# Two gated spectral filters on one core: the second branch's inverse units are divided by output rows, run in halves by kind of product, and the whole plan is written anew

## The chip, the cores and the metric

The kernel runs on one core of one Trainium2 chip. The metric is the time of one execution on the device in microseconds (us), the median of several runs, lower being better.

## What is computed

One image `x` of 2048 rows and 1024 columns goes through two spectral filters with different weights. A gate, one number for each row of the image, mixes the two results.

```python
def _ref(x, w_r, w_i):                       # once with A's weights, once with B's, both on x = A_x
    X = jnp.fft.rfft2(x.astype(jnp.float32), axes=(-2, -1))
    X = X * (w_r + 1j * w_i)                 # 2048 x 513
    return jnp.fft.irfft2(X, s=(2048, 1024), axes=(-2, -1)).astype(jnp.bfloat16)

g = sigmoid((x * gate_w).sum(-1, keepdims=True))
out = g * a + (1 - g) * b
```

## The kernel before

The row of the image is 16 p + n2: partition p holds 16 rows, n2 = 0 to 15. All transforms are matmuls with constant matrices, and every matmul result is evicted from PSUM by ACT (line 417) or DVE (line 418). The stages:

1. **S1, Z, gate.** The columns of x are folded into sums and differences on DVE (`fS`, `fT`, `f2`, line 395). For each n2 a matmul group S1 makes the first part of the transform over the rows, and its eviction Z goes to the buffer TV. A small group `gfold` needs the constants MS, which the DMA `c_MS` brings (ACT's queue), and the gate's weights, which `gwr` reverses on ACT. Its eviction `g8` feeds the groups `gate`, whose rows `zrow` are evicted and summed (`zg`).
2. **D, S2.** Sixteen groups D, number 4 sq + j, transform the columns; they read all of Z. Their evictions Q lie in the ring, 8 cells for each sq. For each sq two groups S2 finish the transform over the rows, evicted as X into the buffer R4: 16 slots s, of which sq covers four, with two parts of 513 each.
3. **Products.** For each branch b (0 is A, 1 is B) and each sq, DVE makes four products of X with the weights (`mul`, `prod`): two kinds (o = 0 with the real weights, o = 1 with the imaginary ones), each in two halves h of two slots. `ploc` says where each product lies. Kind 1 overwrites its weights in WAB. Kind 0 goes into the upper half of TV for A. For B it goes where A's products of kind 1 lay, so it waits until A's units have read those.
4. **Inverse units I.** A wide unit (`stage_iw`, I1W, 32 matmuls) takes half of the slots of one sq and makes a part of all 16 output rows n2. A narrow unit (`stage_i1`, I1, 64 matmuls) takes all slots of one sq and makes one half of the output rows: th = 0 gives n2 0 to 7 (lower), th = 1 gives n2 8 to 15 (upper). `WIDE` lists which (b, sq) are wide. Each unit fills two pairs of PSUM banks, evicted as two tiles V (j = 0, 1) into the ring, 2 of its 28 cells each. From there a DMA of 256 KB, the *turn*, carries the tile across partitions into TV: A's part over Z, B's part over A's products of kind 0. So there are 16 units, 32 evictions V and 32 turns. A ring cell is free again when its turn has landed.
5. **Tail.** For each output row n2, S1A reads A's part and S1B reads B's part of TV, with the gate folded into the constants FM and RM (`sig`, `RA`, `RB`); S1H is both in one group. The eviction G goes to R4, Di2 (or Di) transforms the columns, its eviction `o` goes to WAB, and DVE unfolds in steps u, e and y. A DMA on SP's queue writes each pair of rows. `vkeys` says on which turns a row n2 waits: all turns of wide units, and the turns of narrow units of its own half.

Nothing is scheduled at run time. `Plan` numbers all steps (nodes) in the order in which the program adds them. Three strings, ORDER, ENGS and CELLS, give the order in which they are issued, the engine of each, and the place of each tile in PSUM or ring. A planner wrote these strings beforehand. Each engine runs its steps in that order, and so do the two queues that issue DMAs, POOL and SP. `Sched` sets the waits.

In the order before, the wide units are all of A's and B's sq 3. PE runs the units in the order (b, sq, and half): 0,1,1 | 0,1,0 | 0,0,1 | 0,2,1 | 0,0,0 | 0,2,0 | 0,3,0 | 0,3,1 | 1,0,0 | 1,0,1 | 1,3,1 | 1,2,0 | 1,1,0 | 1,3,0 | 1,1,1 | 1,2,1, the first two ahead of the last two D groups, the first four ahead of the last S2 group. After these come S1A of the rows 2, 0, 3 and 1, and S1B of 3, 2, 1 and 0. The DMA `c_MS` is ACT's second step, `gwr` follows the load of the activation table, and `c_DI` (512 KB of constants for Di) is issued by SP ahead of all turns. Of B's narrow units, SP issues the turn of j = 0 and POOL that of j = 1; POOL issues all turns of wide units.

Of the kernel before, what the change touches and what calls it, by code (L numbers as in the profile page):

```python
# [19 lines left out]
PAIRS = {"warm": 12, "S2": 16, "I1": 64, "I1W": 32, "S25": 8, "gate": 8, "zg": 4, "gm": 8}  # L20
DEPTH = ((0, 2), (2, 4), (4, 6), (6, 8), (8, 10), (10, 12), (12, 14), (14, 16))
ORDER = (
    "020b0h030c000i04010506070n0j080m090f0a0g0d0q0s0e0o0t0r0k0y0w0p0z0u0l24140x15100v251b12111a181h131g1c19261o1e1p1d16271q1f"
    "1r2s28171w1s1u1i1t292v1x1v1j2a1z1m2w1k1y2t2b1n1l22202c232u212y2x2z2d3o3m2e3p3b3n2f3s3c2g3q3t372h3r31382i403u3239422j412q"
    "303v3a33352k343w3x362l493z3y2m434a3d5n3g2n445p3e3i2o473h3f45482p5o3j464o5q3k4p4b3l4h4i4j4e4c5b4f4k4d4g4l5w2r5c5r5x635z59"
    "4q5u4m774r5y644n5i605s5v5a5t4y5l4s6v5j5m4t614u4z5k6a6w50624v6d6b4x6e7n4w6c5d6h655e6f5g5f6i55665h516g56676t686j527o696o6m"
    "6u6k6n7z6r6l6x816p6s7l6q726y82706z7m757188737976747p788b8c7a7s897q7t7b808a7r57837c7e7d587f7g86538454877j857u7h7k7i8u7v7x"
    "8d7w8z7y8i908v918j8w8e8k928x8f938l8y8g8m9b94958h979f969c9u8n8o9g9q988q9v9d9r9h9e9w8p9i9s99a59x8r9a9ja99t9k8saia69l8t9yam"
    "aa9z9ma7aja09nabana1aka89oaoac9palava2apazaeawa3b8aqb0a4axadb9arbab1afaybdasbmb2agatbbahbeb4boaubcbibrbhbnb3bsbfbpbgb5bq"
    "bvb6bub7btbjbwbkbxblbybz")  # L30
ENGS = (
    "sadsadpsasssdasdsasaspdspdapdpadpagdadpagdpadpdadpagdpdapgdadpgadppdagpdadgdpapdagdappgdpappagppgdpagpdgpapgapdgpddpagds"
    "ppappgddpagpdagpaddpgadpagpdapagdpapdaaddpadppdapadapsdpadadpapdagdapgagdgpaddagpdaagpdadpadagdagpdpadagdpagpdagdapadgpa"
    "dagdagpdagdgpadasdagpadgspdagdadagpdgsdpadsdgpadadgagpagspadpspgpppapdpappadpapapddadpdapddapddapdpapdapdpadsdpaddpadsdp"
    "addpaddpadpadpdsapdapdadpdaspdadapdapdpaddpsadasadpdadadpddadddsdddddsds")
CELLS = (
    "071052794002440d28404702486402463204060846204g62402640g027420648g02461204260204406624gij7062402062446086002462460284602a"
    "0244668c026042a264680402ac60402046400824264002c406408248a060424c0460280g424078064867c60046")


def bf16_bits(a):
# [309 lines left out]
def bass_gated_mix__spectral_gfnet__spectral_gfnet__prompt_kernel(  # L351
# [289 lines left out]
    def ploc(b, o, cx, s):  # L641
        if o:
            return WAB, (2 * b + 1 - cx) * WH + s * WP
        if b:
            return WAB, cx * WH + s * WP
        return TV, 16384 + s * 2 * NS + cx * NS

    def prod(b, sq):
        P.key = ("P", b, sq)
        for h in range(2):  # L650
            s0 = 4 * sq + 2 * h
            x = ap(R4, s0 * 2 * NS, [[2 * NS, 2], [NS, 2], [1, NS]])
            r = [("X", s0 + i, c) for i in range(2) for c in range(2)] + [("X5", sq)] + wk[b]
            for o in range(2):
                w = ap(WAB, (2 * b + o) * WH + s0 * WP, [[WP, 2], [(WH, -WH)[o], 2], [1, NS]])
                if o:
                    d, old = w, [("P", b, sq, 0, h)]
                elif b:
                    d, old = ap(WAB, s0 * WP, [[WP, 2], [WH, 2], [1, NS]]), [("P", 0, sq, 1, h)]
                else:  # L660
                    d, old = ap(TV, 16384 + s0 * 2 * NS, [[2 * NS, 2], [NS, 2], [1, NS]]), allf
                P.add("mul", vt(2048), lambda e, w=w, d=d, x=x: [tt(d, x, w, ALU.mult)], r, [("P", b, sq, o, h)], after=old)

    def stage_i1(b, sq, th):
        P.key = ("I", b, sq, th)
        v = [Tile("v", 2), Tile("v", 2)]
        t = [Tile("ps", 2), Tile("ps", 2)]
        pk = [("P", b, sq, o, h) for o in range(2) for h in range(2)]

        def fns():  # L670
# [12 lines left out]
        old = [("P", 0, q, 0, h) for q in range(4) for h in range(2)] if b else allz  # L683
        pt = pit[id(TV)]
        for j in range(2):
            ev("V", 1024, lambda j=j: (rg(v[j], 0, [[1, 1024]]), psl(t[j], 0, [[1, 1024]])),
               [(t[j],)], [(v[j], 0, 2)], alloc=[v[j]])
            dma("turn", ("sp", "pool")[j], lambda j=j: [(AP(TV, (64 * j + sq) * pt + b * 16384 + th * 1024, [[4 * pt, 16], [2048, 8], [1, 1024]]),
                                                         rg(v[j], 0, [[1, 1024]]))], 0.262, 118, [(v[j], 0, 2)], [("V", b, sq, th, j)], after=old)

    def stage_iw(b, sq, a):
        P.key = ("I", b, sq, a)
        v = [Tile("v", 2), Tile("v", 2)]
        t = [Tile("ps", 2), Tile("ps", 2)]

        def fns():
            f = []
            for pr in range(4):
                for c in range(2):
                    for i in range(2):  # L700
                        T, off = ploc(b, pr // 2, pr % 2, 4 * sq + 2 * a + i)
# [5 lines left out]
        pe("I1W", [512] * 8 + [64], fns, [("P", b, sq, o, a) for o in range(2)] + ["SK"], [(t[0],), (t[1],), ("I1", b, sq, a)], alloc=t)  # L707
        old = [("P", 0, q, 0, h) for q in range(4) for h in range(2)] if b else allz
        pt = pit[id(TV)]
        for j in range(2):  # L710
            ev("V", 1024, lambda j=j: (rg(v[j], 0, [[1, 1024]]), psl(t[j], 0, [[1, 1024]])),
               [(t[j],)], [(v[j], 0, 2)], alloc=[v[j]])
            dma("turnw", "pool", lambda j=j: [(AP(TV, (64 * j + 32 * a + sq) * pt + b * 16384, [[4 * pt, 8], [1024, 16], [1, 1024]]),
                                               rg(v[j], 0, [[1, 1024]]))], 0.262, 118, [(v[j], 0, 2)], [("V", b, sq, "w", a, j)], after=old)

    for sq in range(4):
        for j in range(4):
# [39 lines left out]
    allx = [("X", s, c) for s in range(16) for c in range(2)] + [("X5", i) for i in range(4)]  # L757
    oldw = [("P", 1, sq, o, h) for sq in range(2) for o in range(2) for h in range(2)] + \
           [k for b in range(2) for k in wk[b]]

    def tail(ns):
        k = len(ns)
        o, e, y = Tile("o", 2 * k), Tile("e", 2 * k), Tile("y", 2 * k)
        for r, n2 in enumerate(ns):
# [6 lines left out]
                pe("S1H", [128] * 16, lambda n2=n2, t=t: s1inv(n2, t), vkeys(n2), [(t,)], alloc=[t])  # L771
            if k == 1:
                for c in range(2):
                    ev("G", 512, lambda n2=n2, t=t, c=c: (ap(R4, n2 * 1024 + c * 512, [[1, 512]]), psl(t, c * 512, [[1, 512]])),
                       [(t,)], [("G", n2, c)], after=allx)
            else:
                ev("G", 1024, lambda n2=n2, t=t: (ap(R4, n2 * 1024, [[1, 1024]]), psl(t, 0, [[1, 1024]])),
                   [(t,)], [("G", n2, c) for c in range(2)], after=allx)

            def di(c, t, n2=n2):  # L780
                f = []
                for par in range(2):
                    for hh in range(2):
                        l = ap(R4, n2 * 1024 + c * 512 + par * 256 + hh * 128, [[1, 128]])
# [88 lines left out]
```

## Time and profile before

| what | us |
|---|---|
| runs shown | 124.15, 126.17, 126.38 |
| their median | 126.17 |
| span of the profiled execution | 124.9 |
| busy in the span: PE, DVE, ACT, POOL | 103.4, 99.5, 96.5, 41.6 |

The page's header says how long the profiled execution took from its first to its last instruction. That span is 1.3 us below the median of the runs, and one run lies below it. PE is the matmul engine, and a busy PE is not one at its peak. No engine is busy throughout, so the share of each stage matters, not the mean. Times below count from the start of the span.

### The profile page before, as it was taken

Reading aid. Unit: us, or ns where it says so; the run is one execution under the profiler, and the core shown is the slowest. Engines: PE = TensorE matmul, PEld = TensorE weight load, DVE = VectorE, ACT = ScalarE, POOL = GpSimd, SP = SyncE. Lnnn points to the kernel's source line nnn. Section 1 sums busy time; section 2 is a strip of 40 time slices with the busy share of each in tenths; the row PEclk is TensorE's granted clock in tenths of the full one; section 3 lists DMA queues with packets and bytes.
Section 4 is the critical chain, followed back from the end, with each engine's and each line's share of the span. In section 5 each row is a group of like instructions: output and inputs, shape, how many; then the busy total and the mean of one; then the engine's idle time right before and its main releaser. Section 6 shows DMA issues by size and latency. Waiting matters only on the chain.

```text
span 124.9 us, 3644 instructions
## 1 busy us (share of the span) xinstructions
PE 103.4 (83%) x1588; PEld 71.7 (57%) x1588; DVE 99.5 (80%) x134; ACT 96.5 (77%) x111; POOL 41.6 (33%) x74
## 2 busy tenths in 40 slices
PE   6799979999999999785969965896499999999610
PEld 2288836977764556333524322432389999999400
DVE  0479999458699997999999999480307899999991
ACT  4499999466999879994989695673519999999930
POOL 0007699999990003613334331333100000000000
PEclk9999999999999999999999999999859999999975
DMA  4999999999999972898675789889680004444456
GB/s 106 407 419 411 385 336 235 341 338 322 321 293 293 247 212 58 227 168 199 183 182 160 172 205 259 219 190 225 203 243 7 0 5 168 168 173 168 198 220 253
DMA packets 10881, 27.85 MB, mean 223 GB/s; under 512 B 4305, under 2 KB 4305, under 8 KB 10610
## 3 DMA queue, kind: packets, MB, share of 16 engines
q0 software_dynamic: 6688, 15.25, 45.2%
q1 hardware_dynamic: 4032, 12.36, 28.2%
q8 instruction: 12, 0.20, 0.6%
q10 hardware_dynamic: 146, 0.02, 0.1%
q14 instruction: 3, 0.02, 0.1%
HBM read 15.01 MB, written 4.19 MB: 154 GB/s over the span
## 4 chain that ended last, share of the span: by engine, by line
DVE 33%; DMA 22%; PE 22%; ACT 14%; issue 5%; SPq 1%; DVEq 0%; ACTq 0%
PE PS L392 22%; DMA TV<-RING 18%; DVE RING L395 18%; ACT RING L417 9%; DVE WAB L395 9%; DMA WAB<-in_A_x_dram 4%; DVE R L418 3%; ACT R L417 2%; DVE TV L395 2%; DVE RING L418 1%; ACT TV L417 1%; ACT FM L729 1%; ACT WAB L417 1%; SPq L426 1%; DVE WAB L418 0%
## 5 line engine op out<-in xcount | busy, mean ns | idle before, releaser
L417 ACT ACTIVATE RING<-PS 128x1024 bf16<-128x1024 f32 x41 | 40.2, 1026 | 15.0 <-PE PS L392 8.2
L395 DVE TENSOR_TENSOR WAB<-R,WAB 128x2052 bf16<-128x2052 bf16 x24 | 28.1, 1225 | 0.7 <-DMA WAB<-in_B_w_i_dram 0.6
L395 DVE TENSOR_TENSOR RING<-WAB 128x1024 bf16<-128x1024 bf16 (+1 forms) x42 | 23.9, 608 | 5.3 <-DMA WAB<-in_A_x_dram 4.5
L417 ACT ACTIVATE R<-PS 128x1024 bf16<-128x1024 f32 (+2 forms) x29 | 24.6, 937 | 4.3 <-PE PS L392 4.2
L426 POOL DMA_DIRECT2D TV<-RING x26 | 15.2, 586 | 37.1 <-ACT RING L417 20.2
L392 PE MATMUL PS<-WAB,SK 64*32 64x512 bf16 (+1 forms) x576 | 23.4, 377 | 3.4 <-ACT RING L417 3.4
L392 PEld LDWEIGHTS PS<-WAB,SK 64*32 64x32 bf16 (+1 forms) x576 | 10.5, 97 | 15.0 <-ACT RING L417 6.2
L392 PE MATMUL PS<-FM,TV 128*128 128x128 bf16 x128 | 14.5, 237 | 3.1 <-ACT RING L417 3.1
L392 PE MATMUL PS<-DM,TV 128*128 128x256 bf16 x128 | 15.5, 274 | 0.3 <-ACT TV L417 0.3
L392 PEld LDWEIGHTS PS<-FM,TV 128*128 128x128 bf16 x128 | 13.6, 120 | 3.8 <-ACT RING L417 3.8
L418 DVE CAST RING<-PS 128x1024 bf16<-128x1024 f32 x7 | 8.6, 1223 | 9.0 <-PE PS L392 4.9
L418 DVE CAST R<-PS 128x1024 bf16<-128x1024 f32 (+1 forms) x9 | 9.9, 1105 | 6.6 <-PE PS L392 6.5
L392 PEld LDWEIGHTS PS<-DM,TV 128*128 128x128 bf16 x128 | 13.3, 115 | 2.3 <-issue 1.2
L417 ACT ACTIVATE WAB<-PS 128x1024 bf16<-128x1024 f32 (+1 forms) x16 | 14.5, 1014 | 0.2 <-PE PS L392 0.2
L392 PE MATMUL PS<-DI,R 128*128 128x256 bf16 (+1 forms) x128 | 13.4, 260 | 1.1 <-ACT R L417 1.1
L417 ACT ACTIVATE TV<-PS 128x1024 bf16<-128x1024 f32 x14 | 13.3, 1040 | 0.5 <-PE PS L392 0.5
L392 PE MATMUL PS<-TV,RING 128*128 128x256 bf16 (+1 forms) x128 | 12.3, 253 | 1.7 <-DVE RING L395 0.8
L392 PE MATMUL PS<-RM,TV 128*128 128x128 bf16 x128 | 13.4, 222 | 0.0
L392 PEld LDWEIGHTS PS<-RM,TV 128*128 128x128 bf16 x128 | 12.9, 115 | 0.0
L392 PEld LDWEIGHTS PS<-TV,RING 128*128 128x128 bf16 x128 | 10.3, 98 | 4.3 <-DVE RING L395 2.2
L392 PEld LDWEIGHTS PS<-DI,R 128*128 128x128 bf16 x128 | 11.0, 98 | 2.6 <-ACT R L417 1.6
L392 PE MATMUL PS<-TV,SK 64*64 64x512 bf16 x128 | 8.4, 381 | 4.4 <-DVE RING L418 1.8
(41 smaller groups left out, 97.9 us busy)
## 6 DMA issues: line engine op xcount, KB each, us to landing
TV<-RING POOLq DMA_DIRECT2D x26, 256.0 KB, 6.0
WAB<-in_A_x_dram SPq DMA_DIRECT2D x8, 512.0 KB, 7.3
out_dram<-RING SPq DMA_DIRECT2D x7, 512.0 KB, 2.6
TV<-RING SPq DMA_DIRECT2D x6, 256.0 KB, 6.0
WAB<-in_A_w_r_dram POOLq DMA_DIRECT2D x2, 513.0 KB, 9.8
WAB<-in_A_w_i_dram POOLq DMA_DIRECT2D x2, 513.0 KB, 9.0
WAB<-in_B_w_r_dram POOLq DMA_DIRECT2D x2, 513.0 KB, 8.7
WAB<-in_B_w_i_dram POOLq DMA_DIRECT2D x2, 513.0 KB, 12.1
```

Source lines behind the costliest of these rows:

```text
L392: return lambda e: e.matmul(o, l, r, start=start, stop=stop, skip_group_check=True)
L395: return lambda e: e.tensor_tensor(out=o, in0=a, in1=b, op=op)
L417: return [lambda e: e.activation(o, i, ACT.Copy)]
L418: return [lambda e: e.tensor_copy(o, i)]
L426: n = P.add(name, es, lambda e: [lambda q, d=d, s=s: q.dma_start(d, s) for d, s in pairs()], reads, writes, dma=kind, **kw)
L729: P.add("sig", {"act": (0.92, 1.12)}, lambda e, f=f, t=t: [lambda e: e.activation(f, psl(t, 0, [[1, 1024]]), ACT.Sigmoid)], [(t,)], [("gr" ...
```

## The change

Four things change in the program text.

- `WIDE` loses (1, 3). All eight units of branch B are now narrow, so four of them make only lower rows and four only upper rows. `vat` lays B's rows in TV one after the other. A lower turn of B then covers only the place of A's products of sq 0 and 1, an upper turn that of sq 1 to 3 (`dead`).
- A narrow unit is issued as two nodes of 32 matmuls, first the products of kind 0, then those of kind 1, and each waits for its own kind alone. They share their PSUM tiles, and their matmuls are those of before.
- B's products of kind 0 of the slots 8 to 15 go to the lower half of R4, where X of the slots 0 to 7 lay, and not into WAB.
- The inverse rows G of n2 0 to 7 go to the upper half of R4, those of n2 8 to 15 to the upper halves of the first two parts of WAB (`grow`), with the waits of `oldg`. `oldw` no longer names the loads of the weights.

The cut diff:

```diff
-WIDE = ((0, 0), (0, 1), (0, 2), (0, 3), (1, 3))
+WIDE = ((0, 0), (0, 1), (0, 2), (0, 3))
...
         if b:
-            return WAB, cx * WH + s * WP
+            return (WAB, cx * WH + s * WP) if s < 8 else (R4, (2 * s - 16 + cx) * NS)
...
+                elif b and sq > 1:
+                    d = ap(R4, (s0 - 8) * 2 * NS, [[2 * NS, 2], [NS, 2], [1, NS]])
+                    old = [("X", s0 - 8 + i, c) for i in range(2) for c in range(2)] + [("X5", sq - 2)]
...
+    def vat(b, n2):
+        return b * 16384 + (n2 if b else n2 % 8 * 2 + n2 // 8) * 1024
+
+    def dead(b, th):
+        return [("P", 0, q, 0, h) for q in ((0, 1), (1, 2, 3))[th] for h in range(2)] if b else allz
...
-            for pr in range(4):
+            for pr in (2 * o, 2 * o + 1):
...
-        pe("I1", [512] * 8 + [64], fns, pk + ["SK"], [(t[0],), (t[1],), ("I1", b, sq, th)], alloc=t)
+        for o in range(2):
+            pe("I1", [512] * 4 + [64], lambda o=o: fns(o), [("P", b, sq, o, h) for h in range(2)] + ["SK"], [(t[0],), (t[1],)], alloc=t if o == 0 else [])
...
+    def grow(n2, off, n):
+        t, at = (R4, 16 * NS + n2 * 1024) if n2 < 8 else (WAB, (n2 // 4 - 2) * WH + 8 * WP + n2 % 4 * 1024)
+        return ap(t, at + off, [[1, n]])
```

The strings ORDER, ENGS and CELLS are new from end to end. Read against the list of nodes they give these orders, as far as they bear on the text below:

- **Front.** ACT: gw, table, two FN, Z 0, Z 1, gwr, Z 3, `c_MS`, Z 2, Z 5, Z 6, Z 7, g8, Z 4, Z 8, Z 9, Z 13, Z 12, Z 11, Z 15. PE: S1 of 0, 1, 2, 3, 5, 6, 4, 7, then gfold, then S1 of 8, 9, 13, 12, 10, 11, 14, 15, gate 0, gate 2, then D. DVE sets the 8 zeros that `table` reads after the first fold. Two of three `zrow` go from ACT to DVE, and gate 1, gate 3 and the four `zg` come later, among the D groups.
- **D and S2.** PE: D 3, 2, 12, 0, 1, 5, 4, S2 of sq 0, D 6, 7, S2 of sq 0, D 14 and so on. All D and S2 groups now come before the first unit. The last D is D 8; three S2 groups follow it. The first product is (0, 0). Between the first product and the last, DVE also evicts three X and one Q, and one `zrow`, but no V (before: four X, two V).
- **Units on PE:** 0,0,1 | 0,1,0 | 0,1,1 | 0,3,0 | 0,0,0 | 1,1,0 | 0,2,0 | 1,1,1 | 0,3,1 | 0,2,1 | 1,0,0 | 1,3,0 | 1,2,0 | 1,0,1 | 1,3,1 | 1,2,1. The two `gm` groups of the gate stand between the halves of 1,3,0. The last two products are (1, 2), kinds 0 and 1 of h = 1. S1A of the rows 3, 1, 0, 2 and S1B of 1, 2, 3, 0 follow the last unit.
- **V.** DVE evicts one of the two tiles of 1,3,0, both of 1,0,1, and one each of 1,3,1 and 1,2,1, with `RA` and `RB` between them. ACT evicts the other 27.
- **Turns on SP:** 1,3,0 | 1,0,0 | 1,1,0 | 1,2,0, then `c_DI`, then 1,1,1 | 1,0,1 | 1,3,1 | 1,2,1, all j = 0. **On POOL:** 18 turns (the 16 of branch A, and j = 1 of 1,1,0 and 1,0,0), then j = 1 of 1,2,0 | 1,3,0 | 1,0,1 | 1,3,1 | 1,1,1 | 1,2,1.
- **Cells.** Thirteen tiles V stand on places that no turn holds, a fourteenth place is kept for the last tile of 1,2,1, and every other tile waits for an earlier turn. The tiles of 1,3,1 wait for POOL's 16th and 18th turn. The first `y` step (rows 2 and 3), DVE's twelfth step of the tail, takes the cells of that last tile of 1,2,1, so it waits for SP's last turn.

More of the change, by code (lines that the diff above doesn't have):

```diff
@@ L22 @@
 ORDER = (
[L23 to L30, printed above, removed]
+    "02030405060708090a0h0n000m0s0t0y0z14151b1a1h1g0i0b010f0g0o0p0q0u0w0r0j0x0c0v121316101718190k1c0l111e1d1f1p1j1o1x1q1r1w1i"
@@ L667, in stage_i1, with fns @@
         t = [Tile("ps", 2), Tile("ps", 2)]
-        pk = [("P", b, sq, o, h) for o in range(2) for h in range(2)]
-        def fns():
+        def fns(o):
             f = []
-            for pr in range(4):
+            for pr in (2 * o, 2 * o + 1):
                 for c in range(2):
@@ L687, in stage_i1 @@
                [(t[j],)], [(v[j], 0, 2)], alloc=[v[j]])
-            dma("turn", ("sp", "pool")[j], lambda j=j: [(AP(TV, (64 * j + sq) * pt + b * 16384 + th * 1024, [[4 * pt, 16], [2048, 8], [1, 1024]]),
-                                                         rg(v[j], 0, [[1, 1024]]))], 0.262, 118, [(v[j], 0, 2)], [("V", b, sq, th, j)], after=old)
+            dma("turn", ("sp", "pool")[j], lambda j=j: [(AP(TV, (64 * j + sq) * pt + vat(b, 8 * th), [[4 * pt, 16], [(2048, 1024)[b], 8], [1, 1024]]),
+                                                         rg(v[j], 0, [[1, 1024]]))], 0.262, 118, [(v[j], 0, 2)], [("V", b, sq, th, j)], after=dead(b, th))
     def stage_iw(b, sq, a):
@@ L706, in fns @@
             return f
-        pe("I1W", [512] * 8 + [64], fns, [("P", b, sq, o, a) for o in range(2)] + ["SK"], [(t[0],), (t[1],), ("I1", b, sq, a)], alloc=t)
-        old = [("P", 0, q, 0, h) for q in range(4) for h in range(2)] if b else allz
+        pe("I1W", [512] * 8 + [64], fns, [("P", b, sq, o, a) for o in range(2)] + ["SK"], [(t[0],), (t[1],)], alloc=t)
         pt = pit[id(TV)]
@@ L713, in stage_iw @@
             dma("turnw", "pool", lambda j=j: [(AP(TV, (64 * j + 32 * a + sq) * pt + b * 16384, [[4 * pt, 8], [1024, 16], [1, 1024]]),
-                                               rg(v[j], 0, [[1, 1024]]))], 0.262, 118, [(v[j], 0, 2)], [("V", b, sq, "w", a, j)], after=old)
+                                               rg(v[j], 0, [[1, 1024]]))], 0.262, 118, [(v[j], 0, 2)], [("V", b, sq, "w", a, j)], after=dead(b, 0) + dead(b, 1))
     for sq in range(4):
@@ L755, in vkeys, with oldg @@
                 for x in ((("w", 0), ("w", 1)) if (b, sq) in WIDE else ((n2 // 8,),))] + [(("RA", "RB")[b], n2 // 8) for b in bs]
-    allx = [("X", s, c) for s in range(16) for c in range(2)] + [("X5", i) for i in range(4)]
-    oldw = [("P", 1, sq, o, h) for sq in range(2) for o in range(2) for h in range(2)] + \
-           [k for b in range(2) for k in wk[b]]
+    oldw = [("P", 1, sq, o, h) for sq in range(2) for o in range(2) for h in range(2)]
+    def grow(n2, off, n):
+        t, at = (R4, 16 * NS + n2 * 1024) if n2 < 8 else (WAB, (n2 // 4 - 2) * WH + 8 * WP + n2 % 4 * 1024)
+        return ap(t, at + off, [[1, n]])
+    def oldg(n2):
+        if n2 < 8:
+            return [("X", s, c) for s in range(8, 16) for c in range(2)] + [("X5", i) for i in (2, 3)]
+        return [("P", 0, sq, 1, h) for sq in (2, 3) for h in range(2)]
     def tail(ns):
@@ L773, in tail @@
                 for c in range(2):
-                    ev("G", 512, lambda n2=n2, t=t, c=c: (ap(R4, n2 * 1024 + c * 512, [[1, 512]]), psl(t, c * 512, [[1, 512]])),
-                       [(t,)], [("G", n2, c)], after=allx)
-            else:
-                ev("G", 1024, lambda n2=n2, t=t: (ap(R4, n2 * 1024, [[1, 1024]]), psl(t, 0, [[1, 1024]])),
-                   [(t,)], [("G", n2, c) for c in range(2)], after=allx)
+                    ev("G", 512, lambda n2=n2, t=t, c=c: (grow(n2, c * 512, 512), psl(t, c * 512, [[1, 512]])),
+                       [(t,)], [("G", n2, c)], after=oldg(n2))
+            else:
+                ev("G", 1024, lambda n2=n2, t=t: (grow(n2, 0, 1024), psl(t, 0, [[1, 1024]])),
+                   [(t,)], [("G", n2, c) for c in range(2)], after=oldg(n2))
             def di(c, t, n2=n2):
```

24 lines of the change are left out of this document (15 added, 9 removed).

## The prediction

> **What bounds the kernel now.** I cut the span where the work changes hands: the start of the D groups (22.06), the first product (33.64), the end of the last one (78.04, where the next DVE step starts), the first S1B (92.54) and the end of DVE (122.33). The windows view gives each stretch: length, busy time of the five engines with instruction counts, granted clock, DMA share, GB/s.
>
> ```profile
> span 124.9 us, 3644 instructions
> PE 103.4 (83%) x1588; PEld 71.7 (57%) x1588; DVE 99.5 (80%) x134; ACT 96.5 (77%) x111; POOL 41.6 (33%) x74
> ...
> 0.00:22.06 22.06, 18.81 (x180) 12.81 (x181) 16.39 (x26) 18.26 (x23) 10.97 (x23) 1.00 0.94 328
> 22.06:33.64 11.58, 11.58 (x132) 9.50 (x133) 6.95 (x10) 7.49 (x9) 11.58 (x20) 1.00 1.03 333
> 33.64:78.04 44.40, 36.77 (x670) 19.41 (x668) 43.69 (x42) 37.19 (x42) 15.07 (x26) 1.00 0.81 206
> 78.04:92.54 14.50, 10.74 (x256) 6.28 (x257) 5.03 (x7) 7.40 (x8) 3.96 (x7) 0.90 0.85 218
> 92.54:122.33 29.79, 25.54 (x354) 23.69 (x352) 27.47 (x52) 26.13 (x32) 0.00 (x0) 0.96 0.34 131
> ```
>
> PE fills the second stretch (11.58 of 11.58), DVE the third (43.69 of 44.40), DVE and ACT together the fifth. In the fourth no engine is full, and DMA is at 0.85. The chain of waits (start, us, what) tells what the fourth waits for:
>
> ```profile
> 82.06 7.63 DMA TV<-RING
> ...
> 89.78 1.03 ACT RING L417
> 90.86 2.56 PE PS L392 x24
> ```
>
> The timeline (start, us, instruction, idle before it and what ended that) shows the same from PE and DVE:
>
> ```profile
> 78.04 0.69 DVE L395 TENSOR_TENSOR FM<-RM,FM 128x1024 bf16<-128x1024 bf16 x1
> 78.55 5.63 PE L392 MATMUL PS<-WAB,SK 64*32 64x512 bf16 x160 [1.77 <-ACT RING L417]
> 84.37 1.92 PE L392 MATMUL PS<-WAB,SK 64*32 64x512 bf16 x64 [0.19 <-ACT RING L417]
> 87.76 1.22 DVE L418 CAST RING<-PS 128x1024 bf16<-128x1024 f32 x1 [4.06 <-DMA TV<-RING]
> 89.14 1.49 PE L392 MATMUL PS<-FM,TV 128*128 128x128 bf16 x16 [2.85 <-ACT RING L417]
> 90.86 1.89 PE L392 MATMUL PS<-FM,TV 128*128 128x128 bf16 x16 [0.22 <-ACT RING L417]
> 92.54 2.20 PE L392 MATMUL PS<-RM,TV 128*128 128x128 bf16 x32
> ```
>
> After the last product four units remain. Their evictions wait for ring cells, cells wait for turns of some 7.6 us, and S1A waits for PSUM behind those evictions (2.85). S1B starts right behind S1A: it waits for PE, not for landings. From S1B on, 32.3 us remain (92.54 to 124.85). So the end is S1B's start plus the tail.
>
> **The change, term by term.** The sum is made against the profiled execution, span 124.9; the median of the runs is 126.17, and I carry the difference over to it.
>
> *Term 1, the front: +1.5.* The counts of S1, folds and evictions stay. ACT takes in `gwr` and the issue of `c_MS` and gives two `zrow` to DVE:
>
> ```profile
> 1.28 0.37 ACTq L426 DMA_DIRECT2D MS<-c_MS  x1
> 3.09 1.04 ACT L494 ACTIVATE R<-R 1x1024 bf16<-1x1024 bf16 x1
> 7.25 1.94 ACT L417 ACTIVATE TV<-PS 128x1024 bf16<-128x1024 f32 x2 [0.19 <-PE PS L392]
> 9.43 9.31 ACT L417 ACTIVATE TV<-PS 128x1024 bf16<-128x1024 f32 x10 [0.17 <-PE PS L392]
> 18.62 1.09 ACT L417 ACTIVATE FM<-PS 128x512 bf16<-128x512 f32 x2
> ...
> MS<-c_MS ACTq DMA_DIRECT2D x1, 16.0 KB, 4.6
> DM<-c_DM SPq DMA_DIRECT2D x1, 512.0 KB, 13.6
> ```
>
> That is 1.04 + 0.37 - 1.09 = +0.3. The wait is worth more. `gwr` ended at 4.13, well ahead of the first Z; now Z 0, Z 1, `gwr` and Z 3 stand ahead of `c_MS`, which is issued at about 7.25 + 1.9 + 1.0 + 0.3 = 10.5 instead of 1.28. At 4.6 us it lands at 15.1; PE can run `gfold` at about 13.7, as its PSUM is free after Z 5, three evictions of 0.93 later. Behind `gfold` stand all further S1 on PE, and behind `g8` on ACT eight evictions Z. From `g8` on, ACT needs 0.2 + 7 x 0.93 = 6.7 to the last Z (ten take 9.31), and D reads every Z. I take 5.9 us for `c_MS`, between its own 4.6 and the 13.6 of a constant queued under load, much nearer to 4.6 as it is 16 KB on a queue of its own. It lands at 16.4, and D starts at 16.4 + 0.5 + 6.7 = 23.6, 1.5 late. Bounds: 0 (landing hidden) and +9 (13.6 us, D at 31). The zeros for `table` now follow a fold, which costs 0.7 at most and is inside these bounds.
>
> *Term 2, D to the first product: 0.* Before, 11.6. After, nine D and two S2 groups come ahead of the X that the first product needs:
>
> ```profile
> 22.06 5.40 PE L392 MATMUL PS<-DM,TV 128*128 128x256 bf16 x48 [0.35 <-ACT TV L417]
> 27.39 0.61 PE L392 MATMUL PS<-TV,G 128*32 128x512 bf16 x8
> 27.94 1.06 PE L392 MATMUL PS<-RING,SK 64*64 64x512 bf16 x16
> 29.83 0.24 PE L392 MATMUL PS<-MS,FM 128*128 128x1 bf16 x4
> 30.00 0.29 PE L392 MATMUL PS<-RING,SK 128*64 128x2 bf16 x8
> 32.43 1.23 DVE L418 CAST R<-PS 128x1024 bf16<-128x1024 f32 x1 [1.64 <-PE PS L392]
> 33.64 2.37 DVE L395 TENSOR_TENSOR TV<-R,WAB 128x2052 bf16<-128x2052 bf16 x2
> ```
>
> 9 x 0.9 + 2 x 0.95 + 1.2 for the eviction + 0.3 = 11.5. First product at 35.1.
>
> *Term 3, first to last product: -2.2.* DVE is the bound here:
>
> ```profile
> 48.21 3.51 DVE L395 TENSOR_TENSOR WAB<-R,WAB 128x2052 bf16<-128x2052 bf16 x3 [0.64 <-DMA WAB<-in_B_w_i_dram]
> 60.82 15.03 DVE L395 TENSOR_TENSOR WAB<-R,WAB 128x2052 bf16<-128x2052 bf16 x13
> ```
>
> A product or an eviction takes 1.15 (13 in 15.03). The 32 products stay. Six evictions (four X, two V) become four plus one `zrow` (half the columns, taken as 0.7): -2.3 + 0.7. The 0.64 for B's weights goes, since B's first product now follows thirteen of A's and comes well after 48. The new home in R4 has the same shape, so it costs nothing if its readers are done: it waits for products that stand earlier on DVE itself. Bounds: -2.9 and 0 (a product that waits for a unit of A). The last product ends at 77.3.
>
> *Term 4, last product to S1B: -3.3.* Before, 14.5. After: the second half of 1,2,0 (0.95); 1,0,1 and 1,3,1 (1.88 each, three units in 5.63); 1,2,1, whose PSUM is free only when DVE has evicted both tiles of 1,0,1 with `RA` between (1.2 + 0.7 + 1.2 against 1.9 on PE: 1.0 lost); 1.88; four S1A and a wait of 0.2 (3.6). Sum 11.2, so S1B at 88.5. Two covers must hold.
>
> First, ring cells. All D and S2 groups now precede the units: 16 x 0.9 + 8 x 0.95, and 3.4 for four Nyquist groups, two gates and four `zg` (0.29, 0.61, 0.24) make 25.4. With the unit (1.9) and its eviction (0.9) the first tile stands at D + 28.2 = 51.8.
>
> ```profile
> 48.80 1.79 POOL L426 DMA_DIRECT2D TV<-RING  x3 [11.34 <-PE PS L392]
> 71.25 20.10 SPq L426 DMA_DIRECT2D TV<-RING  x6
> ...
> 52.00:60.00 8.00, 5.54 (x104) 2.71 (x107) 8.00 (x8) 5.96 (x8) 2.39 (x4) 1.00 0.89 190
> 75.00:79.00 4.00, 2.23 (x82) 0.97 (x74) 3.73 (x4) 2.53 (x3) 0.83 (x2) 1.00 0.98 240
> ...
> TV<-RING POOLq DMA_DIRECT2D x26, 256.0 KB, 6.0
> DI<-c_DI SPq DMA_DIRECT2D x1, 512.0 KB, 3.4
> RM<-c_RM SPq DMA_DIRECT2D x1, 512.0 KB, 10.3
> ```
>
> So turns begin 3.0 later than at 48.80. A turn is 262 KB: 1.38 us at the 190 GB/s that POOL alone moved, 1.09 at the 240 of POOL and SP together. POOL's 18th turn lands near 51.8 + 6 + 17 x 1.38 = 81.3, and 1,3,1 needs its cell at 82.
>
> Second, landings of the lower rows. SP holds the j = 0 tiles of 1,1,0 and 1,0,0 back behind 1,3,0, whose tiles come at 77. So at 77.3 four lower turns go out on SP and some two remain on POOL; with what moves beside them, eight turns, 9 to 11 us and some 2 to land: 88 to 90, against 88.5. The upper turns end later, and S1A, S1B and the first Di2 cover them. That is the gain: before, S1B came after every unit's eviction had found its cell. Bounds of term 4: -4.3 (DVE costs PE nothing) and +1.5 (no overlap of the queues).
>
> *Term 5, the tail: +0.5.* Counts on DVE and ACT are the same (one eviction swapped). Two new waits: the first Di2, 2 us behind S1B at 90.5, needs `c_DI`, issued near 81 among the turns. It landed in 3.4 on quiet queues; its twin `c_RM` took 10.3 under load. And the first `y` step, some 9 us into the tail, needs SP's last turn: some 17 transfers from 77.3 at 1.1 to 1.38 end between 96 and 101, against 97.5. Bounds 0 and +3.
>
> *Sum:* 1.5 + 0 - 2.2 - 3.3 + 0.5 = -3.5. Span 121.4; median 126.17 - 3.5 = 122.7.
>
> **The rivals.**
> - *`c_MS` is not late* (landing by 14.5, term 1 is +0.3): 121.5 (122.7 - 1.2). For it: 16 KB on a queue of its own. Against it: the loads fill DMA at 0.94 there. The Trainium skill, "DMA: Bandwidth & Descriptors", section "Queues, rings and completion order", speaks for it: each DMA engine goes round its queues a whole packet of typically 9 to 17 descriptors at a time, so eight rows for each engine (128 over 16, an estimate) would go in one turn. The trace of before shows `c_MS` only ahead of most loads, so it does not decide.
> - *The transfers hold S1B and y back.* If SP beside POOL adds no rate (1.38 throughout), lower rows land near 90 (+1.7) and the first `y` waits some 1.5: 126. For it: term 4's second cover has no slack. Against it: 240 GB/s against 190. The same page, section "Issuing engines are not separate DMA queues", holds that issuing from several engines saves only sequencer time; the trace differs, as DMA moved 240 at a share of 0.98 and 190 at 0.89.
> - *Slower: `c_MS` lands as late as `c_DM` did.* Its place is PE's `gfold`, its price is one for one. At 13.6 us from 10.5, D starts at 31.3 and the median is 130.4. It is over 2% slower once `c_MS` takes more than 12 us. For it: W's first loads join it in the queues. Against it: the 4.6.
> - *The gain is partly eaten:* D at 25 to 27 or one cover failing by 2: 124.1 to 126.
>
> **How the numbers follow.** Forecast 0.42 (122.7, most of it below 123.65, the 2% bound); not late 0.14; eaten 0.16; transfers 0.17; slower 0.11. 2% is about what a measurement of this kernel can tell from no change. Faster by over 2%: 0.40 + 0.13 = 0.53; slower 0.11; within 2% 0.36. The range leaves one in ten out on each side: 119.5 (term 1 at 0, term 4 at -4.3, term 3 at -2.9, term 5 at 0: -7 at the very least) to 127.0 (the transfers' case and a late front). It holds both signs; the forecast's own is 121 to 124.
>
> **What would show it.** D starts near 23.6, with PE idle before `gfold` on the DMA of MS; first product near 35, last near 77; no `RING` eviction idle on a DMA for more than 1 us after 77; S1B at 88 to 90; DVE not idle ahead of its first `y`. Wrong if D starts after 27, if S1B waits for landings past 91, or if the tail from S1B is over 34.

## The result, and the profile after

| | median us | runs | ratio to before, 95% |
|---|---|---|---|
| before | 125.70 | 4 (124.15 to 126.38) | |
| changed | 130.49 | 4 (130.28 to 132.93) | 1.043 (1.033 to 1.054) |

The changed kernel is slower, 7.8 us above the forecast of 122.7 and above the range. Executions of the kernel before differ from each other by several us, and the ratios here and below compare undisturbed ones, so they are not the quotients of the medians.

The page of the changed kernel: header, busy times, and the granted PE clock in 40 slices of 3.2 us.

```profile
span 128.5 us, 3773 instructions
PE 104.7 (82%) x1652; PEld 72.6 (57%) x1652; DVE 103.5 (81%) x139; ACT 93.4 (73%) x106; POOL 40.1 (31%) x72
...
PEclk9999995599999999999999999999999999999995
```

Two slices near 20 us now run at half clock; none did there before. The windows view, cut where the prediction cut it (start of D, first product, end of the last product, S1B; the last stretch here runs on to the end of the span), shows where the time lies. Columns as before: length, busy time of PE, PEld, DVE, ACT and POOL, granted clock, DMA share, GB/s.

```profile
0.00:29.52 29.52, 20.25 (x164) 13.91 (x165) 16.72 (x27) 17.21 (x20) 17.92 (x34) 0.88 0.96 328
29.52:41.49 11.97, 11.96 (x132) 9.72 (x136) 8.45 (x11) 7.68 (x8) 8.45 (x15) 1.00 1.03 303
41.49:84.04 42.55, 37.99 (x749) 20.70 (x744) 42.45 (x42) 38.14 (x43) 10.60 (x18) 1.00 0.56 138
84.04:94.93 10.89, 8.77 (x273) 4.97 (x257) 8.34 (x10) 4.17 (x5) 3.18 (x6) 1.00 0.95 245
94.93:128.45 33.52, 25.72 (x355) 23.31 (x352) 27.58 (x52) 26.24 (x32) 0.00 (x0) 0.94 0.55 180
```

Against the first trace of before the stretches changed by +7.46, +0.39, -1.85, -3.61 and +1.21, in sum +3.6. Against this one trace, the gain between the first product and S1B came out about as forecast; the front took it back and more. The chain of waits (start, us, what) names the place:

```profile
8.94 1.92 PE PS L392 x16
10.89 9.76 DMA MS<-c_MS
20.78 3.89 PE PS L392 x24
24.69 4.70 ACT TV L417 x5
29.52 12.91 PE PS L392 x144
```

PE's timeline shows what that load holds up:

```profile
8.94 5.40 PE L392 MATMUL PS<-TV,RING 128*128 128x256 bf16 x48 [0.34 <-DVE RING L395]
20.78 0.34 PE L392 MATMUL PS<-MS,R 1*128 1x4 bf16 x8 [6.44 <-DMA MS<-c_MS]
21.06 6.35 PE L392 MATMUL PS<-TV,RING 128*128 128x256 bf16 x56
29.52 4.64 PE L392 MATMUL PS<-DM,TV 128*128 128x256 bf16 x41 [0.33 <-ACT TV L417]
```

`gfold` stands on PE with all the rest of S1 behind it, so PE is idle for 6.44 us. A second windows view of the same trace, cut at the wait and behind it, gives the clock:

```profile
8.94:14.34 5.40, 5.40 (x48) 4.58 (x48) 5.34 (x9) 5.14 (x6) 2.54 (x5) 1.00 1.03 416
14.34:20.78 6.44, 0.00 (x0) 0.03 (x1) 5.74 (x10) 1.23 (x2) 6.44 (x12) 0.85 1.04 308
20.78:24.20 3.42, 3.42 (x23) 2.51 (x24) 0.00 (x0) 2.12 (x3) 3.42 (x6) 0.50 1.09 304
24.20:27.60 3.40, 3.21 (x43) 2.94 (x41) 1.04 (x1) 2.91 (x4) 3.40 (x7) 0.79 0.97 354
```

Behind the wait PE gets half its clock for 3.4 us and more. The 23 matmuls of that stretch are the 8 small ones of `gfold` and 15 of S1, and these 15 take some 3.1 us; at full clock they take 1.7 (48 in 5.40). So the wait costs PE more than its own length.

In the tail DVE's timeline has one stall on a transfer that was not there before, ahead of the steps `u` of rows 0 and 1:

```profile
93.42 8.92 DMA TV<-RING
```

(chain of waits), and

```profile
100.22 0.76 DVE L395 TENSOR_TENSOR RING<-WAB 128x512 bf16<-128x512 bf16 x2
102.44 0.76 DVE L395 TENSOR_TENSOR RING<-WAB 128x512 bf16<-128x512 bf16 x2 [1.45 <-DMA TV<-RING]
```

(timeline). These steps write into a ring cell that POOL's turn 1,1,1 (j = 1) still reads. Its tile stood near 74, but ORDER issues that turn behind POOL's turn of 1,3,1, at 93.42, and it lands at 102.34.

### The profile page after: what moved, and what is told of

It is laid out like the page before. It is cut to its first block, busy times and chain, and to the rows that moved or that the text cites. A ratio compares the mean times of both kernels' runs of the same rounds, so it can differ in the third digit from the quotient of the medians.

```text
span 128.5 us, 3773 instructions
## 1 busy us (share of the span) xinstructions
PE 104.7 (82%) x1652; PEld 72.6 (57%) x1652; DVE 103.5 (81%) x139; ACT 93.4 (73%) x106; POOL 40.1 (31%) x72
## 4 chain that ended last, share of the span: by engine, by line
DVE 47%; DMA 19%; PE 16%; ACT 7%; issue 6%; SPq 1%; DVEq 0%; POOL 0%
DVE WAB L395 22%; PE PS L392 16%; DVE RING L395 10%; DMA MS<-c_MS 8%; DMA TV<-RING 7%; DVE TV L395 5%; DMA WAB<-in_A_x_dram 5%; DVE RING L418 4%; ACT TV L417 4%; DVE R L395 4%; ACT RING L417 2%; ACT R L417 2%; DVE FM L395 1%; DVE R L418 1%; SPq L426 1%
## 5 line engine op out<-in xcount | busy, mean ns | idle before, releaser
L417 ACT ACTIVATE RING<-PS 128x1024 bf16<-128x1024 f32 x38 | 37.0, 1023 | 13.3 <-PE PS L392 12.9
L395 DVE TENSOR_TENSOR WAB<-R,WAB 128x2052 bf16<-128x2052 bf16 x20 | 23.8, 1225 | 0.1
L392 PE MATMUL PS<-WAB,SK 64*32 64x512 bf16 (+1 forms) x512 | 20.5, 377 | 1.6 <-DVE RING L418 0.6
L417 ACT ACTIVATE WAB<-PS 128x1024 bf16<-128x1024 f32 (+1 forms) x25 | 20.0, 977 | 1.4 <-DVE WAB L395 1.0
L417 ACT ACTIVATE R<-PS 128x1024 bf16<-128x1024 f32 (+1 forms) x20 | 17.6, 947 | 2.2 <-PE PS L392 2.2
L418 DVE CAST RING<-PS 128x1024 bf16<-128x1024 f32 x10 | 12.1, 1220 | 4.7 <-PE PS L392 4.6
L392 PE MATMUL PS<-TV,RING 128*128 128x256 bf16 (+1 forms) x128 | 14.3, 279 | 1.3 <-ACT TV L475 0.8
L426 POOL DMA_DIRECT2D WAB<-in_A_w_r_dram x11 | 6.7, 611 | 11.4 <-DMA WAB<-in_A_x_dram 11.4
L392 PE MATMUL PS<-RING,SK 64*64 64x511 bf16 (+2 forms) x160 | 9.3, 340 | 0.7 <-ACT R L417 0.5
L395 DVE TENSOR_TENSOR TV<-R,WAB 128x2052 bf16<-128x2052 bf16 x8 | 9.6, 1224 | 0.4 <-DVE R L418 0.4
```

The source lines that it names most:

```text
L392: return lambda e: e.matmul(o, l, r, start=start, stop=stop, skip_group_check=True)
L395: return lambda e: e.tensor_tensor(out=o, in0=a, in1=b, op=op)
L417: return [lambda e: e.activation(o, i, ACT.Copy)]
L418: return [lambda e: e.tensor_copy(o, i)]
L426: n = P.add(name, es, lambda e: [lambda q, d=d, s=s: q.dma_start(d, s) for d, s in pairs()], reads, writes, dma=kind, **kw)
```

## Theories, and the first four runs: the late constant

Theory: the changed kernel loses its 7.5 us in the front, because `c_MS` is issued late, among the large loads, and lands 9.8 us after that; the idle time that follows costs PE its clock as well. Rivals: the place of `gwr` and `g8` on ACT, or the new homes and zeros, hold the front back whatever `c_MS` does; or the front doesn't set the end at all.

A few lines added behind the strings ORDER and ENGS move one node behind another in both; where a kernel below is told by `moved`, this is its whole diff. Loads of the constants keep their numbers: 0c is `c_MS`, 0b is gw, 0g the second FN, 0k is `gfold`, 0l is g8, 1l and 23 are Z 10 and Z 15.

```diff
+def moved(node, behind):
+    global ORDER, ENGS
+    n, e = [ORDER[i:i + 2] for i in range(0, len(ORDER), 2)], list(ENGS)
...
+    n.insert(j, node)
+    e.insert(j, g)
```

**`c_MS` first again**, as ACT's second step, all else as changed:

```diff
+moved("0c", "0b")
```

> The changed kernel with one step moved: ACT issues the load of MS second, right behind that of the gate's weights, as the kernel before did. Theory (the late MS costs the front 7.5 us, and the rest of the change gains): MS lands by 6, PE does not wait ahead of gfold, D starts at 22.4 to 23.0 instead of 29.5, and every later stage moves up by the same 6.5 to 7; time 123.9, 1.5% below the kernel before. Rival (the front is late because ACT has the reversal of the gate's weights and the table's wait in it, or what is gained in the front is lost again at the weights' landing and the turns): D no earlier than 26, or time above 126.

Measured: 123.66 us, ratio to before 0.990 (0.984 to 0.995). Its windows:

```profile
0.00:22.31 22.31, 19.46 (x165) 12.57 (x166) 16.45 (x27) 17.10 (x20) 10.86 (x22) 1.00 0.95 329
...
34.26:76.83 42.57, 38.01 (x752) 20.75 (x746) 42.45 (x43) 38.16 (x43) 14.21 (x24) 1.00 0.70 184
76.83:87.71 10.88, 8.77 (x273) 4.96 (x257) 8.33 (x10) 4.16 (x5) 3.17 (x6) 1.00 0.93 241
87.71:121.89 34.18, 25.73 (x355) 23.29 (x353) 27.57 (x52) 26.23 (x32) 0.00 (x0) 0.97 0.54 177
```

One moved DMA gives D 7.2 us earlier (22.31 against 29.52) at full clock, and S1B 7.2 earlier. The two middle stretches are those of the changed kernel within 0.02. So the place of that one load costs 7.2 of the front's 7.5 us. 0.7 of it goes in the tail, which grew from 33.5 to 34.2.

**`c_MS` in the middle**, behind both FN of ACT, issued at 6.20:

```diff
+moved("0c", "0g")
```

> The changed kernel with the load of MS issued behind ACT's two steps FN, near 7.6 us instead of 10.9. Theory (what makes MS late is that its last rows meet the weights' first 16 KB packets, which flow from 16 us on): its rows go out near 11.2 and it lands by 13, before gfold's PSUM is free; D and time as in the run with MS second, 123.9, within 0.5. Rival (a small load on ACT's queue simply takes about 9.8 us whenever the queues are full): it lands at 17.4, D at 26, time 127.

Measured: 123.59 us, ratio 0.992 (0.985 to 1.000); `c_MS` took 6.3 us, landed at 12.54, and `gfold` ran at 14.24 without a wait. Five us later cost nothing; ten cost 7.

**`gfold` last**: `c_MS` stays late, but `gfold` goes behind the last S1 on PE and g8 follows there on ACT (its PSUM place moves along in CELLS):

```diff
+moved("0k", "1l")
+moved("0l", "0k")
+moved("23", "0l")
+CELLS = CELLS[:16] + CELLS[17:30] + CELLS[16] + CELLS[30:]
```

> The changed kernel with MS as late as it is, but with gfold moved on PE behind the last S1, g8 on ACT ahead of Z 15, and PSUM place of gfold unchanged. Theory (only what stands behind gfold on PE and behind g8 on ACT makes the late MS cost anything): MS lands at 20.6 all the same, gfold runs near 21.5, D starts at 23 to 24; time 124.5, within 1 of the run with MS second. Rival (the load itself, or the shortage on the queues, delays the front): D no earlier than 27.

Measured: 123.93 us, ratio 1.001 (0.996 to 1.006). The load is nearly as late as in the changed kernel (8.3 us from 10.67, where 9.8 were expected again), and nobody waits for it:

```profile
17.51 3.47 PE L410 MATMUL PS<-TV,RING 128*128 128x128 bf16 x48 [1.10 <-DVE RING L413]
21.05 0.35 PE L410 MATMUL PS<-MS,R 1*128 1x4 bf16 x8
...
22.67 1.58 PE L410 MATMUL PS<-DM,TV 128*128 128x256 bf16 x13
```

D starts at 22.67. So the late landing costs through what stands behind it: the eight S1 groups behind `gfold` on PE and the evictions behind `g8` on ACT. The run moved both and doesn't tell them apart.

**PE kept busy**: the changed kernel with 30 matmuls of 512 columns on zeros ahead of `gfold`, into a PSUM place that `gfold` overwrites:

```diff
+ORDER, ENGS = ORDER + "c8", ENGS + "p"
+moved("c8", "18")
...
+    pe("keep", [512] * 30, lambda: [mm(psl(gp, 0, [[1, 512]]), rg(warm, 0, [[1, 128]]), rg(warm, 0, [[1, 512]]), True, True) for _ in range(30)],
+       [(warm, 0, 1)], [(gp,)], alloc=[gp])
```

> The changed kernel with thirty matmuls of 512 columns on zeros put ahead of gfold, into gfold's own PSUM bank: 6.5 us of work in PE's wait of 6.4. Theory (of the front's loss of 7.5 us, 1.7 to 1.9 is PE's lowered clock behind the idle stretch, the rest the wait): granted clock 1.0 throughout, S1 8 and 9 take 0.9 each instead of 1.9, D starts at 27.7 instead of 29.5; time 128.7. Rival (the clock costs nothing, as ACT's evictions set the pace behind gfold): time 130.5 as the changed kernel.

Measured: 129.79 us, ratio 1.043 (1.035 to 1.051). PE's timeline, and the window from `gfold` to D with its granted clock:

```profile
14.14 6.42 PE L408 MATMUL PS<-RING 128*128 128x512 bf16 x29
20.50 0.35 PE L408 MATMUL PS<-MS,R 1*128 1x4 bf16 x8
20.78 2.81 PE L408 MATMUL PS<-TV,RING 128*128 128x256 bf16 x32
...
20.50:27.62 7.12, 6.21 (x89) 4.88 (x89) 2.63 (x3) 6.59 (x8) 7.12 (x13) 1.00 1.03 323
```

`gfold` runs nearly as late (20.50 against 20.78), yet the clock stays at 1.00 behind it, and D starts at 27.62, 7.12 behind `gfold` where the changed kernel takes 8.74. So 1.6 us of the front's loss is the clock. S1B comes at 93.00 instead of 94.93, but the end only 0.4 earlier: the stall ahead of `u` grew from 1.45 to 2.96, as the turn of 1,1,1 landed at 101.92 in place of 102.34. So most of what the front gained was lost at a transfer in the tail, and the time is 1.1 above the 128.7 expected.

## Four more runs: the load, the turns, and the two parts of the change

**Why the load takes 9.8 us.** Each row of `c_MS` is a packet of 128 B. The packets, in us, from the trace's table of single packets, with the weights' packets of 16,416 B beside them:

```
kernel     c_MS issued  rows: first  median  90%    last    weights' 16 KB packets
before         1.28      3.93    4.78   5.13   5.32    from 14.98
changed       10.89     14.63   15.54  16.34  19.57    from 15.56, 64 until 19.65, 0.83 each
```

The median row moves 4.7 us after the issue, but the last eight of 128 start between 17.6 and 19.6, and four of the sixteen completions come after 17.1, all while the weights' large packets move. Experiment: the changed kernel, in which POOL's loads of the weights wait for `c_MS`.

```diff
-        dma(name, eng, lambda: prs, mb, 106, [("xl", m) for m in range(0, 8 if name in ("Ws0", "W00") else 14, 2)], [("W", b) + key], after=[("x", m) for m in range(16)] if b else [], n=len(prs))
+        dma(name, eng, lambda: prs, mb, 106, [("xl", m) for m in range(0, 8 if name in ("Ws0", "W00") else 14, 2)] + ["MS"], [("W", b) + key], after=[("x", m) for m in range(16)] if b else [], n=len(prs))
```

> The changed kernel, its late MS unmoved, but POOL issues no load of weights before MS has landed. Theory (the last rows of MS are late because they meet the weights' 16 KB packets): MS lands 6.3 us after its issue, as in the run with MS behind FN, at 17.0 instead of 20.6, and D starts at 24.5 to 25.5. A's weights then land near 40 instead of 33, so the first product starts there, close to 41.5 as in the changed kernel, and the time is 129 to 131. Rival (ACT's queue is slow at that moment whatever else is loaded): MS lands at 20 or later.

Measured: 125.82 us, ratio 1.014 (1.004 to 1.023). The DMA issues of this kernel and PE's timeline:

```profile
MS<-c_MS ACTq DMA_DIRECT2D x1, 16.0 KB, 5.8
```

```profile
16.87 0.33 PE L406 MATMUL PS<-MS,R 1*128 1x4 bf16 x8 [2.49 <-DMA MS<-c_MS]
23.98 6.28 PE L406 MATMUL PS<-DM,TV 128*128 128x256 bf16 x56 [0.33 <-ACT TV L431]
```

Issued at the same time (10.94), beside the same loads of x on SP, the load takes 5.8 us instead of 9.8, and its last row starts at 16.16. So the weights' loads in flight beside it are the cause; whether by the size of their packets or by their number no run told apart. The 9.8 itself varies: with the same neighbours the load took 9.6 in the run with PE kept busy and 8.3 with `gfold` last. The weights' lateness cost less than expected (first product at 36.96, not 40 or later), hence the better time.

**Held-back turns issued early.** `c_MS` first, and besides POOL's turn of 1,1,1 moved up behind the turn of 0,2,1, and SP's turns ordered 1,1,0 | 1,1,1 | 1,0,0 | 1,3,0:

```diff
+moved("0c", "0b")
+moved("7o", "6e")
+moved("8c", "7g")
+moved("7m", "7g")
+moved("70", "7m")
+moved("8c", "70")
```

> The kernel with MS second, with the turns of B issued as their tiles come: SP takes 1,1,0 | 1,1,1 | 1,0,0 ahead of 1,3,0 instead of behind it, and POOL takes 1,1,1 as its 19th turn, ahead of 1,2,0 and 1,3,0, instead of near its last. Theory (the one idle stretch of DVE in the tail, 2.1 us ahead of the first u of rows 0 and 1, is a cell that the held-back turn of 1,1,1 frees late): that stretch is under 0.5, S1B stays at 87.5 to 88, the last turn lands by 95; time 121.6, 3.4% below the kernel before. Rival (the transfers as a whole are late, not their order): the stretch stays at 2, or the lower rows land later and S1B goes past 89; time 123 to 124.

Measured: 122.20 us, ratio 0.983 (0.979 to 0.987), faster than both kernels. The steps `u` run as one group, with no wait:

```profile
93.97 1.43 DVE L415 TENSOR_TENSOR RING<-WAB 128x512 bf16<-128x512 bf16 x4
95.32 2.49 DVE L415 TENSOR_TENSOR WAB<-RING,WAB 128x1024 bf16<-128x1024 bf16 x4
```

From S1B to the end 32.00 remain, against 34.18 with `c_MS` first alone. S1B itself is 1.0 later than there (88.67 against 87.71). PE's timeline shows where:

```profile
78.84 1.04 PE L412 MATMUL PS<-WAB,SK 64*32 64x512 bf16 x27 [0.63 <-DVE RING L438]
80.34 1.27 PE L412 MATMUL PS<-WAB,SK 64*32 64x512 bf16 x37 [0.46 <-issue]
```

A half of unit 1,0,1 stops in its middle, and the profile shows nothing that PE waited for.

**S1B waits for all of B's rows**: `c_MS` first, and the division by rows undone in the reads alone (the part of the line that changes).

```diff
-((n2 // 8,),)
+((0,), (1,))
```

> The kernel with MS second, but every S1B and S1H waits for the turns of both halves of B's rows: the division by rows is undone where it is used. Theory (the division is worth the time from the lower rows' landing to the last one's): S1B starts when the last turn lands, near 97 instead of 87.7, less the 2.1 us that DVE idles later for a turn anyway; time 130 to 131. Rival (the tail's first stretch was bound elsewhere): S1B later, but the end less than 3 us later.

Measured: 132.57 us, ratio 1.068 (1.061 to 1.076).

```profile
85.65 2.30 PE L407 MATMUL PS<-FM,TV 128*128 128x128 bf16 x32
97.25 3.04 PE L407 MATMUL PS<-RM,TV 128*128 128x128 bf16 x27 [9.29 <-DMA TV<-RING]
```

S1B comes 9.54 later (97.25 against 87.71), and nearly all of it reaches the end (span 131.2 against 121.9). The stall of 2.09 ahead of `u` is gone, but behind PE's long wait the granted clock is 0.50 for 3.75 us, and from S1B to the end it still takes 33.9; hence 132.57 and not 130 to 131. With these orders the division by rows keeps S1B from waiting 9.3 us for turns that S1A, S1B and the first Di2 cover. That is not its gain over the kernel before, where S1B waited for PE and not for landings: no run has the old division with orders planned for it.

**Each half waits for both kinds**: `c_MS` first, and the halves' waits by kind undone (the part of the line that changes).

```diff
-[("P", b, sq, o, h) for h in range(2)]
+[("P", b, sq, k, h) for k in range(2) for h in range(2)]
```

> The kernel with MS second, but each half of a narrow unit waits for the products of both kinds, as a narrow unit did before. Theory (the halves matter at 1,2,0, whose first half runs beside the last product): S1B 0.8 to 1.0 later, near 88.6; time 124.5. Rival (the next unit but two waits for DVE's evictions of 1,0,1 anyway, which hides it): S1B within 0.3 of 87.7.

Measured: 125.94 us, ratio 1.007 (1.001 to 1.014); S1B at 90.55, 2.8 late where 0.9 was expected. The place is 1,3,0:

```profile
74.77 1.91 PE L407 MATMUL PS<-R,SK 64*32 64x512 bf16 x32 [3.14 <-DVE WAB L410]
76.61 1.57 PE L407 MATMUL PS<-RM,ZG 128*128 128x128 bf16 x16
```

Its first half now waits for the product of the second kind, and the `gm` groups, which stand between the two halves, wait along; the gate's `FM` and with it `RA` come late on DVE. Here too the clock falls behind the wait: it is 0.57 for the next 3.4 us, and the two groups shown take 1.91 and 1.57 where they take 1.06 and 1.07 with `c_MS` first alone, 1.3 of the 2.8. The direction was expected, this second victim was not.

## Two last traces

The forecast of the fourth stretch rested on one trace of before. The kernel before and the fastest kernel were traced once more.

> The kernel before, unchanged, traced a second time. The prediction's sum was made against one execution with a mean granted clock of 0.968 and a span of 124.9, while other executions of the same kernel show 0.98 to 0.99 and spans near 122.4. Theory: the D groups start at 22.1, the first product at 33.6 and the last product ends near 78 in this trace too, and what an execution at the higher clock has less, some 2 us, lies between the last product and S1B (14.4 in the first trace, at a granted clock of 0.90), with 12 to 13 here and the tail from S1B to the end of the span at 32.0 to 32.3. Then the changed kernel's gain in that stretch is 1.5 to 2 and not 3.5. Rival: the time lies elsewhere (the tail or the product stretch differ by over 1), or the trace repeats the first within 0.5 in each stretch.

```profile
0.00:22.56 22.56, 19.36 (x181) 12.93 (x182) 16.39 (x26) 18.26 (x23) 10.98 (x23) 1.00 0.94 328
22.56:34.14 11.58, 11.58 (x133) 9.50 (x134) 6.96 (x11) 7.50 (x9) 11.58 (x21) 1.00 1.04 333
34.14:77.66 43.52, 36.74 (x670) 19.41 (x668) 43.49 (x42) 37.52 (x42) 15.09 (x26) 1.00 0.79 208
77.66:90.40 12.74, 9.56 (x256) 5.22 (x257) 5.03 (x7) 7.00 (x8) 3.97 (x7) 1.00 0.91 224
90.40:122.46 32.06, 25.29 (x355) 23.46 (x353) 27.48 (x52) 26.13 (x32) 0.00 (x0) 0.93 0.39 146
```

124.26 us. From the last product to S1B this execution takes 12.7 us, not 14.5, at full clock instead of 0.90. The first trace shows why its clock was low:

```profile
89.10:93.40 4.30, 4.04 (x43) 3.78 (x44) 0.00 (x0) 1.02 (x1) 0.54 (x1) 0.60 0.78 227
```

PE had waited 2.85 us ahead of S1A there, and got 0.60 of its clock behind that wait; in the second trace the same wait is 1.57, and the clock stays at 1.00. So 1.8 of the 3.6 that the changed kernel is better there belongs to that one execution, and against the second trace the gain of the stretch is 1.9. Against this trace the changed kernel stands at +7.0, +0.4, -1.0, -1.9 and +1.5, in sum +6.0, inside the interval of its ratio (1.033 to 1.054 is 4.1 to 6.7 us of 124.3).

> The kernel with c_MS early and the held-back turns issued as soon as their tiles stand, unchanged, traced a second time. In its first trace the second half of unit 1,0,1 stopped for about 0.5 in its middle with nothing that PE waited for, and S1B started at 88.67 instead of the 87.7 of the kernel with c_MS early alone. Theory (the turns' transfers in flight there delay PE's own instructions): the stop is there again, S1B at 88.4 to 88.9. Rival (an accident of one execution): no stop, S1B at 87.5 to 88.0 and the span 0.7 to 1.0 shorter than 120.7. Both expect the wait ahead of the steps u of rows 0 and 1 to be 0 to 0.2.

```profile
79.44 1.04 PE L412 MATMUL PS<-WAB,SK 64*32 64x512 bf16 x27 [0.63 <-DVE RING L438]
80.66 1.27 PE L412 MATMUL PS<-WAB,SK 64*32 64x512 bf16 x37 [0.18 <-issue]
...
89.89 1.96 PE L412 MATMUL PS<-RM,TV 128*128 128x128 bf16 x32 [0.73 <-issue]
```

123.69 us in one execution. The kernel before took 124.00 and 124.26 beside it, so the gain is 0.3 to 0.6 us here and not the 1.7% of the first series. `u` has no wait. The first stop is there again after the same 27 matmuls, 0.18 instead of 0.46, and there is a second of 0.73 ahead of S1B, which comes at 89.89: later than either theory said, 0.3 of it because D started 0.6 later and the first stop was shorter, the rest through the second.

The second stop is a wait, though the view says `issue`. S1B needs the turns of B's lower rows. PE's sequencer, which hands PE its instructions, came at 88.39 to a wait for SP's turn of 1,2,0. That turn was issued at 80.90 and landed at 89.69, and the sequencer's next record is at 89.78. In the first trace the same turn had landed at 86.46. So the turns moved up leave S1B no slack.

For the first stop the trace has no such wait. What fits is that PE lacked its own instructions: the single packets show 13 of 16,384 B on a queue named `instruction`, beside 3,350 recorded instructions of PE, 258 for each. The stop ends 1.62 and 1.55 us after the eighth of these packets has ended (78.72 and 79.11). With `c_MS` first alone the eighth ended at 76.03, and PE did not stop there; it stopped 512 instructions further on, for 1.27 us in the first Di2 group, and again went on 1.63 us after such a packet's end. No run moved these packets, so the cause stays open.

## Why the prediction was wrong

- **Term 1 failed**, at the sentence "I take 5.9 us for `c_MS` ... much nearer to 4.6 as it is 16 KB on a queue of its own". Forecast +1.5, measured +7.46. The step that failed is the load's time among its neighbours, and through it PE's wait. The pieces: the issue 0.4 later than reckoned (10.89 against 10.5), the load 3.9 longer (9.76 against 5.9), and 1.7 more from landing to D (8.87 against 7.2; behind `g8` stand seven evictions, as the sum has it, not the eight of the text), of which the run with PE kept busy shows 1.6 as the clock. With the weights held off, the load takes 5.8: the figure fits a load among x alone. What I left out is that POOL's weight loads start within its flight. The upper bound of 9 held it, and the rival "slower" was this mechanism at 13.6 us and 130.4; I gave it 0.11 because 4.6 was the nearest row by size, where the row nearest by circumstance was 13.6. That 130.4 lies so near the measured 130.49 is luck: D started 1.8 sooner than that rival has it, and the stretches behind it took 1.1 more than forecast.
- **The clock behind the wait** was in no term. I priced PE's idle time one for one, though the trace of before already had a granted clock of 0.60 behind a wait of 2.85.
- **The rival "not late"** fell: the load landed at 20.65, not by 14.5. By the Trainium skill, "DMA: Bandwidth & Descriptors", section "Queues, rings and completion order", a DMA engine drains a whole packet from one queue's ring before it turns to the next, so eight rows in one turn were possible. In the trace the last eight rows start up to 3 us behind the 90% mark. Which rows share an engine it does not record, so what broke the reckoning, the size of a turn or the turn of the others, stays open.
- **Term 2** (0): 11.97 against 11.5, wrong by 0.5.
- **Term 3** (-2.2): 42.55 against 42.2 forecast; -1.85 against the first trace, -1.0 against the second. The new home R4 cost nothing: DVE is busy for 42.45 of 42.55.
- **Term 4** (-3.3): the stretch came out at 10.89 against 11.2, the closest of all. Both covers held. Before, ACT's evictions between the last product and S1B waited 4.9 us for turns; in the changed kernel they wait for none. And the last turn of the lower rows landed at 93.41, 1.5 ahead of S1B, while the transfers ran at 245 GB/s where 240 were assumed, so the rival of the transfers fell for S1B. (Whether 240 against 190 is due to the second issuer or to more turns in flight, no run told apart.) But half of the difference came from the first trace of before, whose stretch is 1.8 longer than in the second. A granted clock of 0.90 in that row was the sign, and I quoted it without asking whether the stretch is always so. So the size was in part luck.
- **Term 5** (+0.5): +1.2 (+1.5 against the second trace), inside its bounds and through another wait. Neither `c_DI` (landed at 95.55, its first reader at 96.72 did not wait) nor SP's last turn (landed at 103.62, the first `y` at 105.52) held anything; POOL's held-back turn of 1,1,1 did, and with the turns moved up the stall was gone.
- The other terms, with D where the run with `c_MS` first has it (+0.25), give a span of 124.9 + 0.25 - 5.0 = 120.1; measured is 121.9. Of the 1.8, 1.4 are the tail (34.18 against 32.3 + 0.5, its stall ahead of `u` being 2.09), the rest terms 2 and 3 (0.4 each), less 0.3 that term 4 did better. And the ratio of that run is 0.990, though its span is 3.0 below that of the first trace: that trace was 2.4 slower than the second one of the same kernel (124.9 against 122.5). So even with `c_MS` first the change is worth 1%, where the forecast had 2.8%.

## What to carry to other kernels

A small constant is not cheap by its size: ask which large transfers will be in flight between its issue and its landing, and which engine's whole queue stands behind its first reader; move either the issue to the front or the reader back; with either, D started within 0.6 us of its old place here. Price PE's idle time ahead of dense work with the slow clock that follows it: in these traces it followed waits of 2.85 us and more. Before a gain is read from one stretch of one trace, look at that stretch in a second trace, above all where its granted clock is below the others'.

## What had not been expected of the hardware

- A load of 16 KB on a queue of its own took 5.0 us at the start, 6.3 issued at 6.2, 5.8 at 10.9 without the weights' packets, and 8.3 to 9.8 at 10.6 to 10.9 with them.
- After 6.44 us without matmuls the granted clock was 0.50 for the next 3.4 us. It fell behind waits of 2.85 (before, first trace), 3.14 (halves waiting for both kinds) and 9.29 us (S1B waiting for all rows) too, and not behind 2.49 (weights behind `c_MS`). The Trainium skill, "TensorE: Matmul & The Clock Gate", section "Why this matters for your kernels", warns of such a drop after idle gaps of over some 3 us. The traces agree, with 2.85 as the shortest, and filler matmuls kept the clock at 1.00.
- In two traces PE stopped inside a group of 64 matmuls after the same 27, for 0.46 and 0.18 us, with no wait that the profile shows. Both stops ended about 1.6 us after an instruction packet had.
